# A fused attention and long-convolution kernel: a factored inverse transform, 1/sqrt in one pass, and output copies on ScalarE

## The chip, the cores and the metric

The kernel runs on one core of a Trainium2 chip. The metric is the device time of one execution in microseconds (us), as the median of several runs. The kernel before takes 247.82 us (3 runs, 247.66 to 248.04). All traces here have one core; the "granted clock" beside a run is the mean TensorE clock as a share of full speed, 0.989 for the profiled run of before. PE is the matmul engine, PEld its weight loads, DVE the vector engine, ACT the scalar engine, POOL is GpSimd. "L264" is line 264 of the kernel that is being profiled, so the same statement has slightly different line numbers in different kernels.

## The reference

```python
# q, k, v: (8 batches, 8 heads, 576, 64);   D = 64, S = 576, d_model = 512
kv  = einsum('bhsd,bhse->bhde', k, v)
out = einsum('bhsd,bhde->bhse', q, kv)
x   = out / sqrt(mean(out * out, -1) + 1e-6) * g_norm        # -> (8, 576, 512)
x1, x2, x3 = split(x @ w_proj, 3)                             # 512 x 1536
conv = irfft(rfft(x2) * rfft(filter_fft), n=576)              # along the sequence
y   = (x1 * conv * x3) @ w_out                                # 512 x 512
```

## The kernel before

The program loops over eight batches, and the work of batch b+1's attention (`att_o`, `att_r`, `att_x`, `fold`) is interleaved with batch b's transforms and projections. The forward and inverse transforms are matmuls against tables of cosines and sines; the radix-3 structure of 576 is used on the forward side (`fold`), not yet on the inverse. With cuts marked:

```python
def att_r(b, j):                     # 1/sqrt of the mean square, as exp(-0.5 * ln(.))
    r2 = ps_tile("ps_r2")
    ...                              # matmul: sums of squares into r2
    nc.scalar.activation(out=s['lr'][:, j % 2]..., in_=r2[...], func=AF.Ln, scale=1.0 / D, bias=bias_eps)
    if j % 2:
        nc.scalar.activation(out=s['rstd'][:, j - 1:j + 1], in_=s['lr'], func=AF.Exp, scale=-0.5)

def att_x(b, jp):                    # x = o * rstd, DVE, both inputs bf16 in SBUF
    nc.vector.tensor_mul(out=s['x'][:, r], in0=s['o'][:, r], in1=s['rstd'][:, r])
def fold(b, jp): ...                 # seven short DVE operations on x

def fft(b, g):
    ...                              # matmuls into a PSUM tile xp
    if g < 2:                        # tpw on DVE (PSUM input), the sum Y on POOL
        nc.vector.tensor_mul(out=t_[:n, 0], in0=xp[:n], in1=HH[:n, g, 1:3])
        nc.vector.tensor_mul(out=t_[:n, 1], in0=xp[:n], in1=HH[:n, g, 0:2])
        nc.gpsimd.tensor_add(out=Y[...], in0=t_[:n, :, 0], in1=t_[:n, :, 1])
        return
    nc.vector.tensor_mul(out=Y[:, 4:6], in0=xp[...], in1=HM)      # "the product Y"; frees xp

def inv(b, dcs):
    for h in (1, 0):
        for i, dc in enumerate(dcs):
            for g in range(3):       # three matmuls of 288 columns
                nc.tensor.matmul(p_[h][:, i], Y[...], IV[:n, 2 * g + h], start=(g == 0), stop=(g == 2))
    nc.scalar.copy(out=os_, in_=p_[1])
    nc.vector.tensor_add(out=u[:, :, 0:TH], in0=p_[0], in1=os_)
    nc.vector.tensor_sub(out=u[:, :, TH:S], in0=p_[0][:, :, ::-1], in1=os_[:, :, ::-1])
    nc.vector.tensor_mul(out=st[b]['yg'][:, d2], in0=u, in1=g13[:, d2])

def outp(b, c0, ev=None):            # output matmuls, then the copy from PSUM
    if c0 == 0 and not ev: nc.vector.tensor_copy(out=ot, in_=pp)
    else:                  nc.scalar.copy(out=ot[:, 0:n], in_=pp[:, 0:n])
```

In the traces here each engine takes its instructions one after another, in the order in which they were laid out. That order isn't the order of the Python text: a scheduler lays it out when the program is built, except where `keep_in_program_order` pins it. PSUM tiles come from a small shared pool, so a matmul into a new tile waits until an earlier tile has been read.

## Time and profile before

| what | before |
|---|---|
| time, median | 247.82 us |
| span of the profiled run | 246.6 us |
| busy share PE / DVE / ACT / POOL | 91 / 77 / 63 / 37 % |
| batch period, mean of five (starts of L264, 68.20 to 194.35) | 25.23 us (one short and one long: 25.34) |
| TensorE idle in a steady batch | 0.12 us |
| chain that ended last | PE 78 %, DVE 10 %, ACT 7 % |

The busy share of the whole span is an average over start, steady state and end. The period and the idle time within a batch say more: TensorE has nothing to spare, so what lengthens its in-order path lengthens the kernel. The period alternates between 24.8 and 25.9 us, because one output step is done for two batches at once. The lines themselves are in the prediction.

### The profile page before, as it was taken

Reading aid. Unit: us, or ns where it says so; the run is one execution under the profiler, and the core shown is the slowest. Engines: PE = TensorE matmul, PEld = TensorE weight load, DVE = VectorE, ACT = ScalarE, POOL = GpSimd, SP = SyncE. Lnnn points to the kernel's source line nnn. Section 1 sums busy time; section 2 is a strip of 40 time slices with the busy share of each in tenths; the row PEclk is TensorE's granted clock in tenths of the full one; section 3 lists DMA queues with packets and bytes.
Section 4 is the critical chain, followed back from the end, with each engine's and each line's share of the span. In section 5 each row is a group of like instructions: output and inputs, shape, how many; then the busy total and the mean of one; then the engine's idle time right before and its main releaser. Section 6 shows DMA issues by size and latency. Waiting matters only on the chain.

```text
span 246.6 us, 4887 instructions
## 1 busy us (share of the span) xinstructions
PE 225.6 (91%) x1964; PEld 133.9 (54%) x1964; DVE 190.7 (77%) x337; ACT 154.8 (63%) x231; POOL 90.8 (37%) x103
## 2 busy tenths in 40 slices
PE   4977896867999999999999999999999999999990
PEld 1433353434576657655766576557665766557520
DVE  6739866899698779876887888796779777958560
ACT  2856337981677767785679467946794679543430
POOL 7963992670193019400950086000700070007010
PEclk9999999997999999999999999999999999999998
DMA  6999999994099129914992389340033003400156
GB/s 68 166 196 238 211 194 196 192 180 50 4 142 211 43 64 135 211 49 112 104 185 85 88 98 177 100 129 3 4 85 85 3 0 88 128 0 3 39 151 193
DMA packets 45559, 27.17 MB, mean 110 GB/s; under 512 B 22274, under 2 KB 40706, under 8 KB 45538
## 3 DMA queue, kind: packets, MB, share of 16 engines
q0 software_dynamic: 40256, 17.70, 56.7%
q1 hardware_dynamic: 5122, 8.92, 13.2%
q8 instruction: 15, 0.25, 0.4%
q10 hardware_dynamic: 160, 0.26, 0.4%
q14 instruction: 6, 0.05, 0.1%
HBM read 33.69 MB, written 9.44 MB: 175 GB/s over the span
## 4 chain that ended last, share of the span: by engine, by line
PE 78%; DVE 10%; ACT 7%; issue 2%; ACTq 0%; DVEq 0%
PE ps_x L430 19%; PE ps_out L479 10%; PE ps_x L381 6%; PE ps_invo L454 5%; PE ps_inve L454 5%; PE ps_w L529 4%; PE ps_qT L247 3%; PE ps_o L264 3%; PE ps_x L387 3%; PE ps_x L372 3%; ACT sq L265 2%; PE ps_r L281 2%; PE ps_kv L223 2%; PE ps_x L375 2%; PE ps_X L407 2%
## 5 line engine op out<-in xcount | busy, mean ns | idle before, releaser
L430 PE MATMUL ps_x<-x,wp 128*128 128x288 bf16 x512 | 67.8, 286 | 0.2 <-ACT lr L282 0.2
L413 POOL TENSOR_TENSOR Y<-tpw 128x1024 bf16<-128x1024 f32 (+1 forms) x16 | 37.7, 2359 | 64.5 <-PE ps_r L281 39.7
L430 PEld LDWEIGHTS <-wp 128*128 128x128 bf16 x512 | 49.8, 98 | 14.0 <-issue 1.3
L265 ACT ACTIVATE sq<-ps_o 128x576 bf16<-128x576 f32 x32 | 20.6, 652 | 18.0 <-PE ps_o L264 18.0
L70 POOL DMA_DIRECT2D km<-in_k_dram x9 | 7.9, 873 | 63.2 <-PE ps_kv L223 63.2
L282 ACT ACTIVATE lr<-ps_r,bias_eps 128x576 f32<-128x576 f32 x32 | 23.4, 746 | 7.5 <-PE ps_r L281 7.4
L479 PE MATMUL ps_out<-wo,yg 128*128 128x512 bf16 x112 | 26.4, 379 | 0.7
L436 DVE TENSOR_TENSOR g<-ps_x,x 128x576 bf16<-128x576 f32 x32 | 24.1, 752 | 3.5 <-PE ps_x L430 2.3
L434 ACT CAST x<-ps_x 128x576 bf16<-128x576 f32 x32 | 20.6, 643 | 8.4 <-PE ps_x L430 8.4
L454 PEld LDWEIGHTS <-Y 128*128 128x128 bf16 (+1 forms) x192 | 19.0, 101 | 10.7 <-issue 3.1
L411 DVE TENSOR_TENSOR tpw<-ps_X,HH 128x1024 f32<-128x1024 f32 (+1 forms) x16 | 19.6, 1222 | 3.4 <-PE ps_X L409 2.5
L457 ACT COPY os<-ps_invo 128x576 f32<-128x576 f32 x14 | 9.0, 640 | 20.9 <-DVE u L460 16.3
L270 ACT ACTIVATE osb<-ps_o,g_col 128x576 bf16<-128x576 f32 x28 | 20.8, 741 | 0.0
L251 DVE COPY qT<-ps_qT 128x1152 bf16<-128x1152 bf16 x16 | 11.4, 752 | 11.1 <-PE ps_qT L247 11.1
L412 DVE TENSOR_TENSOR tpw<-ps_X,HH 128x1024 f32<-128x1024 f32 (+1 forms) x16 | 19.4, 1214 | 0.0
L285 ACT ACTIVATE rstd<-lr 128x1152 bf16<-128x1152 f32 x16 | 18.6, 1165 | 0.5
L479 PEld LDWEIGHTS <-yg 128*128 128x128 bf16 x112 | 10.9, 97 | 12.4 <-issue 1.9
L292 DVE TENSOR_TENSOR x<-osb,rstd 128x1152 bf16<-128x1152 bf16 x16 | 12.3, 766 | 6.9 <-ACT rstd L285 6.9
L381 PE MATMUL ps_x<-wp,ab 128*128 128x512 bf16 x64 | 15.5, 381 | 1.5 <-DVE ab L310 1.5
L454 PE MATMUL ps_invo<-IV,Y 128*128 128x288 bf16 (+1 forms) x84 | 13.7, 299 | 2.4 <-DVE g L436 1.6
L529 PE MATMUL ps_w<-kvblk,ind 128*128 128x512 bf16 x37 | 12.1, 469 | 3.8 <-DVE ind L103 3.4
L264 PE MATMUL ps_o<-qT,kvblk 128*128 128x288 bf16 x64 | 12.9, 288 | 2.8 <-DVE kvblk L232 1.7
(170 smaller groups left out, 395.4 us busy)
## 6 DMA issues: line engine op xcount, KB each, us to landing
out_dram<-ot SPq DMA_DIRECT2D x28, 256.0 KB, 3.3
qb<-in_q_dram POOLq DMA_DIRECT2D x16, 288.0 KB, 7.5
km<-in_k_dram POOLq DMA_DIRECT2D x7, 512.0 KB, 7.6
vm<-in_v_dram POOLq DMA_DIRECT2D x7, 512.0 KB, 9.7
wp<-in_moe_w_proj_dram POOLq DMA_DIRECT2D x3, 512.0 KB, 12.1
out_dram<-ot SPq DMA_DIRECT2D x10, 128.0 KB, 3.1
km<-in_k_dram POOLq DMA_DIRECT2D x2, 256.0 KB, 5.8
kt<-in_k_dram POOLq DMA_DIRECT2D x8, 64.0 KB, 6.7
```

The lines of the kernel that those rows point to most:

```text
L264: nc.tensor.matmul(op[:, h, 0:TH], kvblk[b % 2][:, j], s['qT'][:, 2 * (j % 2) + j // 2, h * TH:(h + 1) * TH], start=True, stop=True)
L265: nc.scalar.activation(out=s['sq'][:, j].rearrange("p (a b) -> p a b", a=2), in_=op[:, :, 0:TH], func=AF.Square)
L270: nc.scalar.activation(out=o_, in_=op[:, :, 0:TH], func=AF.Copy, scale=g_col)
L282: nc.scalar.activation(out=s['lr'][:, j % 2].rearrange("p (a b) -> p a b", a=2), in_=r2[:, :, 0:TH], func=AF.Ln, scale=1.0 / D, bias=bias_eps)
L381: nc.tensor.matmul(pp[:, h], ab[:, j, h * SB:h * SB + P], wp[:, j, DM:2 * DM], start=(j == 0), stop=(j == NDC - 1))
L413: nc.gpsimd.tensor_add(out=Y[:n, 2 * g:2 * g + 2], in0=t_[:n, :, 0], in1=t_[:n, :, 1])
L430: nc.tensor.matmul(pp[:, h, 0:TH], w_, x[:, j, h * TH:(h + 1) * TH], start=(j == 0), stop=(j == NDC - 1))
L434: nc.scalar.copy(out=x1, in_=pp[:, :, 0:TH])
L436: nc.vector.tensor_mul(out=st[b]['g13'][:, dc].rearrange("p (a b) -> p a b", a=2), in0=pp[:, :, 0:TH], in1=x1)
L454: nc.tensor.matmul(p_[h][:, i], Y[:n, 2 * g + h, dc * P:(dc + 1) * P], IV[:n, 2 * g + h], start=(g == 0), stop=(g == 2))
L479: nc.tensor.matmul(pp[:, cc], yg[:, dc, c * P:(c + 1) * P], wo[:, dc], start=(dc == 0), stop=(dc == NDC - 1))
L529: tc.keep_in_program_order(nc.tensor.matmul(pp[:, 0], ind, kvblk[1].rearrange("p a b -> p (a b)"), start=True, stop=True))
```

## The change

The intent: TensorE is the full engine, so give it less to do. The inverse of length 576 is factored: the matmuls now have 192 and 96 columns and give three parts of a third of the output each. DVE adds the short part (from the 96 columns, mirrored) to the two outer ones in one operation, and POOL makes the middle third, the short part less both outer ones, in two. The product that ends a batch's second half is moved behind the next batch's first projection (`fins[1]()`). To pay for the DVE work, an output copy goes to ScalarE, and to pay for that, 1/sqrt becomes one ScalarE pass.

```diff
-    preload_act_table_set("natural_log_exp_and_others")
+    preload_act_table_set("abs_reciprocal_sqrt_and_small")
@@ kv:  the second state eviction of the first batch moves to ScalarE
-            if b == 0:
+            if b == 0 and j0 == 0:
@@ att_r
-        activation(out=s['lr'][:, j % 2], in_=r2, func=AF.Ln, scale=1.0 / D, bias=bias_eps)
-        if j % 2:
-            activation(out=s['rstd'][:, j - 1:j + 1], in_=s['lr'], func=AF.Exp, scale=-0.5)
+        activation(out=s['rstd'][:, j], in_=r2, func=AF.Abs_reciprocal_sqrt, scale=1.0 / D, bias=bias_eps)
@@ inv
-                for g in range(3): matmul(p_[h][:, i], Y[...], IV[:n, 2 * g + h], ...)     # 288 columns
+                for g in (1, 2):   matmul(p_[h][:, i, 0:SB], Y[...], IV[:, 2 * g + h, 0:SB], ...)   # 192
+                matmul(p_[h][:, i, SB:TH], Y[:N1, h, cs], IV[:N1, h, 0:SB // 2], ...)               # 96
+        eng = eng or nc.gpsimd
+        eng.tensor_add(out=w3[:, :, 1], in0=u3[:, :, 0], in1=u3[:, :, 2])
+        eng.tensor_sub(out=w3[:, :, 1], in0=u3[:, :, 1], in1=w3[:, :, 1])
+        nc.vector.tensor_add(out=w3[:, :, 0:3:2], in0=u3[:, :, 0:3:2], in1=u3[:, :, 1:2].to_broadcast(...))
-        nc.vector.tensor_mul(out=st[b]['yg'][:, d2], in0=u, in1=g13[:, d2])
+        def fin(): nc.vector.tensor_mul(out=st[b]['yg'][:, d2], in0=w, in1=g13[:, d2])
+        return fin
@@ outp
-            if c0 == 0 and not ev: nc.vector.tensor_copy(out=ot, in_=pp)
-            else:                  nc.scalar.copy(out=ot[:, 0:n], in_=pp[:, 0:n])
+            nc.scalar.copy(out=ot[:, 0:n], in_=pp[:, 0:n])
@@ loop over batches
         proj2(b)
+        if b: fins[1]()
...
-        for dp in (0, 2): inv(b, (dp, dp + 1))
+        fins = [inv(b, (dp, dp + 1)) for dp in (0, 2)]
+        fins[0]()
```

Cut: a `warm(2)` left out at the start, and the last batch, which does all of this on DVE.

More of the change, by code (lines that the diff above doesn't have):

```diff
@@ L176 @@
         nc.scalar.activation(out=IV[:, 2 * c], in_=a_, func=AF.Sin, scale=cosb[:, 2 + h:3 + h], bias=cosb[:, h:h + 1])
-    tc.keep_in_program_order(nc.scalar.preload_act_table_set("natural_log_exp_and_others"))
+    tc.keep_in_program_order(nc.scalar.preload_act_table_set("abs_reciprocal_sqrt_and_small"))
     g_col = consts.tile([P, 1], FP32)
@@ L276, in att_r @@
             s['rstd'] = work.tile([P, NDC, S], BF16, name="rstd", tag="rstd")
-        if j % 2 == 0:
-            s['lr'] = work.tile([P, 2, S], FP32, name="lr", tag="lr")
         r2 = ps_tile("ps_r2")
@@ L281, in att_r @@
             nc.tensor.matmul(r2[:, h, 0:TH], ind, s['sq'][:, j, h * TH:(h + 1) * TH], start=True, stop=True)
-        nc.scalar.activation(out=s['lr'][:, j % 2].rearrange("p (a b) -> p a b", a=2), in_=r2[:, :, 0:TH], func=AF.Ln,
-                             scale=1.0 / D, bias=bias_eps)
-        if j % 2:
-            nc.scalar.activation(out=s['rstd'][:, j - 1:j + 1], in_=s['lr'], func=AF.Exp, scale=-0.5)
+        nc.scalar.activation(out=s['rstd'][:, j].rearrange("p (a b) -> p a b", a=2), in_=r2[:, :, 0:TH],
+                             func=AF.Abs_reciprocal_sqrt, scale=1.0 / D, bias=bias_eps)
     def att_x(b, jp):
@@ L436, in proj13, with inv @@
                 nc.vector.tensor_mul(out=st[b]['g13'][:, dc].rearrange("p (a b) -> p a b", a=2), in0=pp[:, :, 0:TH], in1=x1)
-    def inv(b, dcs):
+    def inv(b, dcs, eng=None):
         Y, g13 = st[b]['Y'], st[b]['g13']
@@ L451, in inv @@
             for i, dc in enumerate(dcs):
-                for g in range(3):
-                    n = N1 if g == 0 else P
-                    nc.tensor.matmul(p_[h][:, i], Y[:n, 2 * g + h, dc * P:(dc + 1) * P], IV[:n, 2 * g + h],
-                                     start=(g == 0), stop=(g == 2))
+                cs = slice(dc * P, (dc + 1) * P)
+                for g in (1, 2):
+                    nc.tensor.matmul(p_[h][:, i, 0:SB], Y[:, 2 * g + h, cs], IV[:, 2 * g + h, 0:SB],
+                                     start=(g == 1), stop=(g == 2))
+                nc.tensor.matmul(p_[h][:, i, SB:TH], Y[:N1, h, cs], IV[:N1, h, 0:SB // 2], start=True, stop=True)
         os_ = work.tile([P, 2, TH], FP32, name="os", tag="os")[:, 0:m]
@@ L460, in inv, with fin @@
         nc.vector.tensor_sub(out=u[:, :, TH:S], in0=p_[0][:, :, ::-1], in1=os_[:, :, ::-1])
+        eng = eng or nc.gpsimd
+        w = work.tile([P, 2, S], BF16, name="w", tag="w", bufs=2)[:, 0:m]
+        u3, w3 = (t.rearrange("p j (m r) -> p j m r", m=3) for t in (u, w))
+        eng.tensor_add(out=w3[:, :, 1], in0=u3[:, :, 0], in1=u3[:, :, 2])
+        eng.tensor_sub(out=w3[:, :, 1], in0=u3[:, :, 1], in1=w3[:, :, 1])
+        nc.vector.tensor_add(out=w3[:, :, 0:3:2], in0=u3[:, :, 0:3:2], in1=u3[:, :, 1:2].to_broadcast([P, m, 2, SB]))
         d2 = slice(dcs[0], dcs[0] + m)
-        nc.vector.tensor_mul(out=st[b]['yg'][:, d2], in0=u, in1=g13[:, d2])
+        def fin():
+            nc.vector.tensor_mul(out=st[b]['yg'][:, d2], in0=w, in1=g13[:, d2])
+        return fin
     yt = {}
@@ L469, in o_rows, with outp @@
         return bass.AP(tensor=out.tensor, offset=out.offset + (b * S + t0[0]) * DM, ap=[[3 * DM, 64]] + two + [[1, DM]])
-    def outp(b, c0, ev=None):
+    def outp(b, c0):
         if c0 < 4 or b % 2:
@@ L486, in outp @@
             n = 2 if c0 < 4 else 1
-            if c0 == 0 and not ev:
-                nc.vector.tensor_copy(out=ot, in_=pp)
-            else:
-                nc.scalar.copy(out=ot[:, 0:n], in_=pp[:, 0:n])
+            nc.scalar.copy(out=ot[:, 0:n], in_=pp[:, 0:n])
             for i in range(2):
@@ L516, in last @@
         for dc in range(NDC):
-            inv(b, (dc,))
+            inv(b, (dc,), nc.vector)()
             if dc < 2:
-                outp(b - 1, 2 * dc, nc.scalar.copy)
+                outp(b - 1, 2 * dc)
         act, dve = nc.scalar.copy, nc.vector.tensor_copy
@@ L536 @@
         kv(0, 2 * jj, 2 * jj + 2)
-        warm(2)
         att_o(0, 2 * jj)
@@ L549 @@
         proj2(b)
+        if b:
+            fins[1]()
         if b == 0:
@@ L602 @@
             del st[b - 1]
-        for dp in (0, 2):
-            inv(b, (dp, dp + 1))
+        fins = [inv(b, (dp, dp + 1)) for dp in (0, 2)]
+        fins[0]()
 _INS = ['q', 'k', 'v', 'g_norm', 'moe_w_proj', 'moe_filter_fft', 'moe_w_out']
```

## The prediction

> **What bounds the kernel now.** I read the page's busy shares first, then the busy time by stage, then the groups of instructions, then the order of time around the joint between two batches. On the page:
>
> ```profile
> span 246.6 us, 4887 instructions
> PE 225.6 (91%) x1964; PEld 133.9 (54%) x1964; DVE 190.7 (77%) x337; ACT 154.8 (63%) x231; POOL 90.8 (37%) x103
> ```
>
> TensorE leads, but a share over the span mixes start, steady state and end, so I cut the span at the starts of the inverse transform. Columns: window, length, then busy time (instructions) of PE, weight loads, DVE, ACT, POOL:
>
> ```profile
> 0.00:30.00 30.00, 22.66 (x176) 9.95 (x176) 21.42 (x68) 15.41 (x25) 21.86 (x46) 1.00 1.18 175
> 83.36:109.14 25.78, 25.66 (x240) 15.90 (x239) 21.75 (x36) 18.76 (x27) 9.32 (x8) 1.00 0.74 110
> 109.14:134.04 24.90, 24.77 (x233) 15.78 (x234) 19.87 (x34) 17.62 (x27) 9.32 (x8) 1.00 0.82 125
> ```
>
> In a steady batch TensorE idles 0.12 of 25 us: what shortens its work shortens the batch, and any new wait on its in-order path lengthens it. DVE, ACT and POOL have 4, 7 and 15 us to spare per batch. The groups of the instructions that change or show a price:
>
> ```profile
> L282 ACT ACTIVATE lr<-ps_r,bias_eps 128x576 f32<-128x576 f32 x32 | 23.4, 746 | 7.5 <-PE ps_r L281 7.4
> L265 ACT ACTIVATE sq<-ps_o 128x576 bf16<-128x576 f32 x32 | 20.6, 652 | 18.0 <-PE ps_o L264 18.0
> L285 ACT ACTIVATE rstd<-lr 128x1152 bf16<-128x1152 f32 x16 | 18.6, 1165 | 0.5
> L413 POOL TENSOR_TENSOR Y<-tpw 128x1024 bf16<-128x1024 f32 x8 | 18.9, 2362 | 62.3 <-PE ps_r L281 39.7 <-PE ps_X L404 19.1 <-DVE tpw L412 3.5
> L462 DVE TENSOR_TENSOR yg<-u,g 128x1152 bf16<-128x1152 bf16 x14 | 10.6, 758 | 0.5
> L488 DVE COPY ot<-ps_out 128x1024 f32<-128x1024 f32 x6 | 7.3, 1225 | 6.5 <-PE ps_out L479 6.5
> ```
>
> The chain that ended last gives TensorE's spacing: six inverse matmuls (288 columns) take 0.74 us, 0.1235 each; sixteen projection matmuls of 288 take 1.96; eight of 512 take 1.73, 0.216 each. That is about 2 ns plus 0.417 ns per column.
>
> Last, DVE against POOL in the first batch, in order of time (start, duration):
>
> ```profile
> 47.31 2.37 POOL L413 TENSOR_TENSOR Y<-tpw 128x1024 bf16<-128x1024 f32 x1 [2.24 <-DVE tpw L412]
> 49.32 0.98 DVE L292 TENSOR_TENSOR x<-osb,rstd 128x1152 bf16<-128x1152 bf16 x1
> 50.33 3.55 DVE L302 TENSOR_TENSOR d__687<-x 128x768 bf16<-128x768 bf16 x1
> 51.09 2.37 POOL L413 TENSOR_TENSOR Y<-tpw 97x1024 bf16<-97x1024 f32 x1
> ```
>
> The subtraction L302 takes 0.55 us everywhere else; here it takes 3.55 and ends 0.42 after POOL's add does. x takes 0.98 instead of 0.76 when it starts 0.36 before a POOL add ends. In the steady batches no DVE instruction with two SBUF inputs meets a POOL add: there the second add runs 98.82 to 101.17, DVE's next such instruction starts at 101.63, held off by the output copy L488 before it.
>
> **What the Trainium skill says.** *SBUF — State Buffer*, "Who interferes with whom": a DVE instruction with two SBUF inputs and a GpSimd instruction that reads SBUF exclude each other for the whole instruction; one with an input in PSUM is free. The two cases above agree (3.55 against 0.55), and products with a PSUM input run beside the same adds at their usual 1.21. *GPSIMD Engine Reference*, "Elementwise — side-by-side cycle accounting": about 2.6 cycles per element with two inputs; the trace has 2.36 us for 1024 elements, 2.3 ns each. *TensorE: Matmul & The Clock Gate*, "Back-to-back issue gap": columns / 2.4 GHz + 2.5 ns; agrees with the spacing above. The same section gives 81 ns for 128 columns with a weight load each; the table transposes (128x128 loads, 128 columns) take 0.36 us for six here, 60 ns, so the trace decides and loads stay hidden down to about there. *ScalarE: Activation LUTs*, "What ACT_TABLE_LOAD costs": every function has one price per element, and a pointer operand adds 93 ns; L282 against L265 (746, 652) agrees.
>
> **The change part by part.**
> Inverse: per batch 24 matmuls of 288 columns (24 x 0.1235 = 2.96 us) become 16 of 192 (0.0825) and 8 of 96 (0.042): 1.66 us. A load limit of 60 ns on the 96-column ones would add 0.15. Saving 1.3 us per batch, all on TensorE: 9.1 us for the seven batches outside the last.
> Middle third: for each of two pairs per batch, POOL does two operations on 384 elements, DVE one on 768. An estimate from the 2.36 us add and the skill's per-element rate: 0.9 to 1.0 us per POOL operation, 4 us per batch. DVE's is priced by L302: 0.55, 1.1 per batch, against the 1.22 output copy that leaves it.
> 1/sqrt: four passes with a bias pointer, about 0.74 each, replace 4 x 0.746 + 2 x 1.165: ACT falls by 2.3 us per batch and takes a 1.01 us output copy. ACT is not the bound; but in the start it is on the path. There the second x begins at 23.66, after lr (20.63 to 22.00) and rstd (22.04 to 23.20), and the second state eviction waits on DVE until 18.32. Without the two Exp passes and with that eviction on ACT at about 17.2, x begins near 21.2. Start: -2.4 us. The later start-up chain (filter products on ACT and DVE) is unchanged and should pass this on.
> End: four single inverses with everything on DVE. Per column block DVE takes 0.46 + 0.45 + 0.25 + 0.25 + 0.46 plus some of a 0.35, about 2.1 us against 1.36 between the last two products before. It eats the 1.3 us that TensorE saves there: +0.4.
> Gross: 247.8 - 9.1 - 2.4 + 0.4 = 236.7, if nothing new waits.
>
> **What waits anew: the joint.** The static order of the changed kernel has, on DVE: both u of pair 1, w, both u of pair 2, product 1, w, product 2, and only then the two qT copies of the next batch. In the trace of before TensorE meets that copy here:
>
> ```profile
> 91.75 1.42 DVE L251 COPY qT<-ps_qT 128x1152 bf16<-128x1152 bf16 x2 [1.30 <-PE ps_qT L247]
> 93.00 0.42 PE L264 MATMUL ps_o<-qT,kvblk 128*128 128x288 bf16 x2
> ```
>
> Count from the start of the inverse (83.36). Before, the copy starts at 8.4 and L264 at 9.64. After, TensorE is there at 8.34. rstd comes 1.2 us earlier, so the folds end at 1.5 and the first u pair at 3.1; pair 2 (single os buffer, 0.64 us of ACT between) ends at 5.2. Free of the lock, POOL ends its second pair at 5.2 + 0.16 + 2 x 1.0 + 0.1 = 7.5, product 2 ends at 8.3, the copy at 9.0: TensorE stands 0.7 us (0.4 after even batches, whose inverse starts later). With the lock, w, two POOL operations and the product of each pair are serial: 2 x (0.5 + 2.0 + 0.7) = 6.4 us from 3.1 plus gaps of 0.4, then the copy 0.7: 10.6, a stall of 2.2, more than the 1.3 saved.
>
> **What waits anew: the third block.** The output copy that held x off is gone from DVE. x is ready 2 us earlier, at 99.5 in the old clock, and meets the POOL add until 101.17. The static order now also puts the seven folds (1.9 us) in front of the Y product that frees the PSUM tile which L430 takes at 103.76. 101.2 + 0.65 + 1.9 + 1.15 = 104.9: a stall of 1.2 to 1.5 in each of six batches. Without the lock it ends at 103.2, no stall.
>
> **Rivals.**
> (a) All hidden: 236.7. For it: TensorE was the only full engine and the deferred product shows that the joint was thought of. Against: the copy behind product 2.
> (b) POOL in series but hardly blocked: five joints x 0.5, the first joint (its product 1 stands before pair 2) +1, the last +0.3: 240.5. For it: the two lock cases are from one batch, and POOL on bf16 is not in this trace; at 0.6 us per operation the joint almost closes.
> (c) Lock at the joint: 236.7 + 5 x 2.1 + 3 + 1 = 251.
> (d) Lock there and in the third block: + 6 x 1.4 = 259.6. For it: the arithmetic above. Against: DVE might come first at some meetings, and each figure rests on overlaps of some tenths.
>
> **Range and chances.** By the trace alone I would lean to (c) or (d). But they need several meetings to fall badly, and POOL's duration is an estimate on which a third of the stall hangs. I weigh (a) 0.12, (b) 0.28, (c) 0.33, (d) 0.27, with spread around each. The middle is 248.5; eight in ten lie between 238.5 and 260. Faster by over 2% (under 242.9): 0.28; within 2%: 0.36; slower (over 252.8): 0.36.
>
> **What would show it.** The inverse groups at 0.083 and 0.042 spacing, 1.66 us per batch (right up to 1.8). The new ACT group near 740 ns. POOL operations on 384 elements at 0.9 to 1.0 when unblocked, longer in some instances. L264 after the joint waiting 0.4 to 2.2 us on the qT copy. x of the third block stretched to over 2 us and a projection matmul waiting on the Y product. The prediction is wrong if these waits are absent (then 237), if the mean POOL operation is under 0.6, or if the start gains nothing because a load lands late.

## The result, and the profile after

The changed kernel is correct and takes 255.17 us (4 runs, 254.42 to 256.17) against 247.79 us for before (4 runs). The ratio is 1.0299, with a 95 % interval of 1.0255 to 1.0343: slower. All ratios in this text are the mean time of one kernel's fast runs over that of the other's in the same rounds, so they are not quite the ratios of the medians quoted. The profiled spans are 254.2 and 246.6 us.

The head of the profile page, and the chain that ended last, by engine:

```profile
span 254.2 us, 4875 instructions
PE 214.6 (84%) x1932; PEld 130.0 (51%) x1960; DVE 208.6 (82%) x355; ACT 143.5 (56%) x223; POOL 119.2 (47%) x131
...
DVE 45%; PE 25%; POOL 12%; ACT 5%; DMA 5%; issue 5%; DVEq 0%; POOLq 0%
```

TensorE has about 11 us less to do, as intended (28 matmul records are missing from this trace, 1932 against 1960 weight loads, so the true figure is somewhat smaller), and the span is 7.6 us longer. The chain has left TensorE: it was 78 % of it before, it is 25 % now, and DVE and POOL carry 57 %. Busy time by stage, cut again at the starts of the inverse (the columns are those of the same view in the prediction):

```profile
86.53:113.75 27.22, 24.59 (x238) 15.45 (x239) 24.59 (x40) 17.56 (x26) 13.67 (x12) 1.00 0.71 104
113.75:139.25 25.50, 23.30 (x230) 15.14 (x233) 22.57 (x33) 16.40 (x26) 13.66 (x12) 1.00 0.80 122
```

TensorE now idles 2.2 to 2.6 us a batch (missing records count as idle; the two waits named below make 1.8 to 2.3 of it) where it idled 0.12, and DVE is busy 22.6 to 24.6 us where it was busy 19.9 to 21.8. The groups that changed or showed a price:

```profile
L280 ACT ACTIVATE rstd<-ps_r,bias_eps 128x576 bf16<-128x576 f32 x32 | 23.3, 742 | 11.8 <-PE ps_r L279 11.8
L288 DVE TENSOR_TENSOR x<-osb,rstd 128x1152 bf16<-128x1152 bf16 x16 | 21.1, 1317 | 2.7 <-ACT rstd L280 2.6
...
L469 DVE TENSOR_TENSOR yg<-w,g 128x1152 bf16<-128x1152 bf16 x14 | 14.8, 1056 | 5.3 <-POOL w L464 4.7
```

A mean hides what goes on here. yg, with the same shape as before (758 ns), has a mean of 1056: its median is still 758, its longest instance takes 1455. x has a mean of 1317 for the same operation that took 766 before: its median is 760, its longest 2293. Something stretches some instances. What TensorE waited for, from the view of waits (total, times, longest):

```profile
PE ps_o L264 <- DVE qT L251: 7.2, 6, 2.2
PE ps_x L426 <- DVE Y L415: 6.1, 6, 1.1
...
PE ps_x L426 <- DVE FX L210: 2.4, 1, 2.4
```

None of the three is in that view of before. They are the three places of the whole story: the joint between two batches (L264 on the copy qT), the third block of a batch (L426 on the product Y), and the start (L426 on the table copy FX).

**The joint.** The timeline of the changed kernel from the inverse of one batch (starts at 113.75) to the first attention product of the next; start, duration, engine, and in brackets the idle time before it. Only rows of DVE and POOL are shown, and the one of TensorE at the end:

```profile
116.51 0.56 DVE L465 TENSOR_TENSOR w<-u 128x768 bf16<-128x768 bf16 x1
116.55 1.28 POOL L463 TENSOR_TENSOR w<-u 128x384 bf16<-128x384 bf16 x1 [11.63 <-DVE u L459]
...
117.93 0.75 DVE L459 TENSOR_TENSOR u<-ps_inve,os 128x576 bf16<-128x576 f32 x1
118.79 0.91 POOL L463 TENSOR_TENSOR w<-u 128x384 bf16<-128x384 bf16 x1
...
118.86 1.45 DVE L469 TENSOR_TENSOR yg<-w,g 128x1152 bf16<-128x1152 bf16 x1 [0.18 <-POOL w L464]
119.78 1.31 POOL L464 TENSOR_TENSOR w<-u,w 128x384 bf16<-128x384 bf16 x1
120.24 1.26 DVE L465 TENSOR_TENSOR w<-u 128x768 bf16<-128x768 bf16 x1
121.60 0.76 DVE L469 TENSOR_TENSOR yg<-w,g 128x1152 bf16<-128x1152 bf16 x1
122.28 1.42 DVE L251 COPY qT<-ps_qT 128x1152 bf16<-128x1152 bf16 x2
123.08 0.40 PE L264 MATMUL ps_o<-qT,kvblk 128*128 128x288 bf16 x2 [0.74 <-DVE qT L251]
```

Read it as a relay. w and POOL's first addition start together at 116.5, and POOL takes 1.28 instead of 0.91. The u at 117.93, which reads PSUM, runs beside POOL at its usual 0.75. Then yg and POOL's addition start within 0.07 us: yg takes 1.45. POOL's next one takes 1.31 beside it, then w takes 1.26. The second yg (0.76) still stands in the queue, and only then is DVE free for the copy that TensorE is waiting for. From 116.51 to 122.28 DVE's operations on SBUF alone and POOL's have taken turns.

**The third block.** DVE's order before the change (the folds follow from 129.31):

```profile
126.37 1.22 DVE L488 COPY ot<-ps_out 128x1024 f32<-128x1024 f32 x1 [1.09 <-PE ps_out L479]
127.51 0.75 DVE L292 TENSOR_TENSOR x<-osb,rstd 128x1152 bf16<-128x1152 bf16 x1
128.18 1.22 DVE L419 TENSOR_TENSOR Y<-ps_X,HM 128x1024 bf16<-128x1024 f32 x1
```

And in the changed kernel, some 6 us after the joint above:

```profile
129.14 2.36 POOL L409 TENSOR_TENSOR Y<-tpw 97x1024 bf16<-97x1024 f32 x1
129.85 2.27 DVE L288 TENSOR_TENSOR x<-osb,rstd 128x1152 bf16<-128x1152 bf16 x1 [0.19 <-ACT rstd L280]
...
134.05 1.22 DVE L415 TENSOR_TENSOR Y<-ps_X,HM 128x1024 bf16<-128x1024 f32 x1
...
135.32 2.12 PE L426 MATMUL ps_x<-x,wp 128*128 128x288 bf16 x16 [1.08 <-DVE Y L415]
```

x ends at 132.12, 0.62 after POOL's addition does at 131.50; its work takes 0.76 where nothing meets it, so most of the 2.27 us was standing. The cut lines between x and Y are the seven folds, 1.9 us in all. Y is what frees the PSUM tile that the projection matmul needs.

**The start.** DVE and TensorE near the first projections:

```profile
27.56 1.15 PE L426 MATMUL ps_x<-x,wp 128*128 128x288 bf16 x8
...
29.09 1.23 DVE L318 TENSOR_TENSOR ff<-fa,fc 128x1024 bf16<-128x1024 f32 x1 [3.74 <-DMA fc<-in_moe_filter_fft_dram,fidx]
...
30.80 0.29 DVE L210 COPY FX<-ps_ft 64x256 bf16<-64x256 bf16 x1
...
31.14 4.57 PE L426 MATMUL ps_x<-x,wp 128*128 128x288 bf16 x24 [2.43 <-DVE FX L210]
```

TensorE is at the projections at 27.56 instead of 30.03, so the gain of the shorter 1/sqrt arrives there. But DVE's next instruction, ff, waits for a gathered load until 29.09, and behind it stand two table copies whose data has long been ready and which free a PSUM tile. TensorE has run into a queue that it used to arrive at just late enough not to notice.

The queue takes back the 2.47 us, and a second loss comes on top. The 24 projection matmuls behind the wait take 4.57 us. In e12, an experiment below with the same start, they take 3.10 after nearly the same wait:

```profile
30.59 3.10 PE L426 MATMUL ps_x<-x,wp 128*128 128x288 bf16 x24 [2.08 <-DVE FX L210]
```

The granted clock differs: from 31 to 36 us it is 0.68 in the changed kernel and 1.00 in e12 and in before. Among the seven kernels with this start, the three with 4.5 to 4.8 us (changed, e7, e11) have 0.68 to 0.72 there, after waits of 2.0 to 3.7 us; the four with 3.10 have 1.00, after 1.3 to 2.1 us. Whether the wait brings the lower clock on isn't shown: e12 waited 2.08 us and kept the clock, e11 waited 2.03 and did not. The wait and the clock together make the filter's transform start 1.6 us later than before (35.55 for 33.96).

The 7.6 us of span add up from the starts of L264: up to the first joint 2.2 us are lost (70.36 against 68.20), in the five periods after it 5.2 us (26.27 against 25.23 each), and 0.3 in the rest. In a period the inverse saves 1.2 us (2.98 to 1.70 and 1.81 by turns), the joint costs 0.99 (7.2 less the first 2.25, over five) and the third block 1.05; 0.2 us remain for smaller waits.

### The profile page after: what moved, and what is told of

It reads as the page before. It is cut to its first block, busy times and chain, and to the rows that moved or that the text cites. A ratio compares the mean times of both kernels' runs of the same rounds, so it can differ in the third digit from the quotient of the medians.

```text
span 254.2 us, 4875 instructions
## 1 busy us (share of the span) xinstructions
PE 214.6 (84%) x1932; PEld 130.0 (51%) x1960; DVE 208.6 (82%) x355; ACT 143.5 (56%) x223; POOL 119.2 (47%) x131
## 4 chain that ended last, share of the span: by engine, by line
DVE 45%; PE 25%; POOL 12%; ACT 5%; DMA 5%; issue 5%; DVEq 0%; POOLq 0%
PE ps_x L426 14%; DVE x L288 6%; DVE yg L469 6%; DMA fc<-in_moe_filter_fft_dram,fidx 5%; POOL w L463 4%; DVE tpw L408 4%; DVE tpw L407 4%; PE ps_out L487 3%; DVE Y L415 3%; DVE w L465 3%; POOL w L464 3%; ACT rstd L280 3%; DVE u L458 3%; DVE u L459 2%; DVE g L432 2%
## 5 line engine op out<-in xcount | busy, mean ns | idle before, releaser
L426 PE MATMUL ps_x<-x,wp 128*128 128x288 bf16 x512 | 69.7, 290 | 9.2 <-DVE Y L415 6.1
L426 PEld LDWEIGHTS <-wp 128*128 128x128 bf16 x512 | 50.3, 99 | 26.2 <-issue 12.5
L463 POOL TENSOR_TENSOR w<-u 128x384 bf16<-128x384 bf16 x14 | 15.7, 1124 | 76.1 <-DVE u L459 76.1
L280 ACT ACTIVATE rstd<-ps_r,bias_eps 128x576 bf16<-128x576 f32 x32 | 23.3, 742 | 11.8 <-PE ps_r L279 11.8
L487 PE MATMUL ps_out<-wo,yg 128*128 128x512 bf16 x99 | 25.8, 379 | 0.7
L495 ACT COPY ot<-ps_out 128x1024 f32<-128x1024 f32 (+1 forms) x17 | 15.9, 937 | 14.0 <-PE ps_out L487 14.0
L288 DVE TENSOR_TENSOR x<-osb,rstd 128x1152 bf16<-128x1152 bf16 x16 | 21.1, 1317 | 2.7 <-ACT rstd L280 2.6
L469 DVE TENSOR_TENSOR yg<-w,g 128x1152 bf16<-128x1152 bf16 (+1 forms) x18 | 16.6, 922 | 5.4 <-POOL w L464 4.7
L264 PE MATMUL ps_o<-qT,kvblk 128*128 128x288 bf16 x64 | 12.8, 287 | 9.6 <-DVE qT L251 7.2
L79 POOL DMA_DIRECT2D qb<-in_q_dram x16 | 12.6, 786 | 7.3 <-DMA wp<-in_moe_w_proj_dram 4.1
L464 POOL TENSOR_TENSOR w<-u,w 128x384 bf16<-128x384 bf16 x14 | 15.1, 1080 | 1.1
L279 PE MATMUL ps_r<-sq,ind 128*128 128x288 bf16 x64 | 13.1, 286 | 1.4 <-ACT osb L270 0.8
```

The lines of the kernel that those rows point to most:

```text
L280: nc.scalar.activation(out=s['rstd'][:, j].rearrange("p (a b) -> p a b", a=2), in_=r2[:, :, 0:TH], func=AF.Abs_reciprocal_sqrt, scale=1.0 ...
L426: nc.tensor.matmul(pp[:, h, 0:TH], w_, x[:, j, h * TH:(h + 1) * TH], start=(j == 0), stop=(j == NDC - 1))
L463: eng.tensor_add(out=w3[:, :, 1], in0=u3[:, :, 0], in1=u3[:, :, 2])
L464: eng.tensor_sub(out=w3[:, :, 1], in0=u3[:, :, 1], in1=w3[:, :, 1])
L469: nc.vector.tensor_mul(out=st[b]['yg'][:, d2], in0=w, in1=g13[:, d2])
L487: nc.tensor.matmul(pp[:, cc], yg[:, dc, c * P:(c + 1) * P], wo[:, dc], start=(dc == 0), stop=(dc == NDC - 1))
```

## The experiments

Twelve kernels ran, on two chips, each beside runs of the kernel before. "Period" is the mean of the five steps from the third batch's first L264 to the last batch's. The granted clock over a whole run scatters (0.978 to 0.985 in the four runs of the changed kernel), and some of the scatter of the times goes with it: in e11 the run at 0.995 took 246.16 us and the one at 0.977 took 249.58.

| run | what it is | median us (before, same rounds) | ratio, 95 % interval |
|---|---|---|---|
| e1 | whole change but the inverse | 251.47 (248.11) | 1.0152, 1.0104 to 1.0200 |
| e2 | changed, tables first at the start | 253.27 (248.11) | 1.0216, 1.0148 to 1.0284 |
| e3 | changed, products behind qT | 250.76 (248.11) | 1.0146, 1.0073 to 1.0220 |
| e4 | changed, four folds behind Y | 253.39 (248.11) | 1.0223, 1.0130 to 1.0316 |
| e5 | before, output copies alone | 245.60 (247.93) | 0.9906, 0.9834 to 0.9978 |
| e6 | before, 1/sqrt alone | 259.48 (247.93) | 1.0490, 1.0409 to 1.0571 |
| e7 | changed, Y right behind x | 248.86 (247.93) | 1.0019, 0.9942 to 1.0096 |
| e8 | changed, all three orders | 240.55 (247.93) | 0.9692, 0.9624 to 0.9760 |
| e9 | e1 with the two orders that apply | 241.62 (247.66) | 0.9761, 0.9730 to 0.9793 |
| e10 | e8 with the middle third on DVE | 240.65 (247.66) | 0.9716, 0.9689 to 0.9743 |
| e11 | changed, middle third on DVE | 247.80 (247.66) | 0.9996, 0.9940 to 1.0053 |
| e12 | changed, POOL only writes (wrong result) | 246.62, one run (247.66) | none |

All but e12 gave the right result. One run each of e1 and e4 is left out of the ratios.

### e1: the change without its inverse

```diff
-    (new inv, fins)
+    (inv of the kernel before, product straight from u)
```

> The changed kernel with the old inverse put back (no middle third, no GpSimd work, product straight from u); everything else of the change stays. Theory (the loss is the inverse's DVE/GpSimd side): batches go back to about 25.3 us between the first attention products of neighbouring batches (26.4 after, 25.3 before), the waits on qT and on Y vanish (under 0.2 us a batch), and the time is 247 to 249 us: the before-time, less about 1.3 us gained by ScalarE in the first batch, plus the 1.6 us that the start got longer. Rival (the output copies or the 1/sqrt on ScalarE hold something up): 252 us or more, with a period over 26 us.

The theory fell here. I had put the loss on the inverse. The time lies between the theory's 247 to 249 and the rival's 252, but the period is the rival's. Without it the wait on qT is gone, but the third block still waits 6.3 us on Y, six times 1.05, and the kernel is 1.5 % slower than before with a period of 26.14 us. So of the 3 % about half has nothing to do with the inverse, its matmuls or its GpSimd work.

### e5 and e6: the two ScalarE parts, each alone on the kernel before

```diff
 e5:
-            if c0 == 0 and not ev: nc.vector.tensor_copy(out=ot, in_=pp)
-            else:                  nc.scalar.copy(out=ot[:, 0:n], in_=pp[:, 0:n])
+            nc.scalar.copy(out=ot[:, 0:n], in_=pp[:, 0:n])
 e6:
-        Ln pass, and an Exp pass for every second one
+        activation(out=s['rstd'][:, j], in_=r2, func=AF.Abs_reciprocal_sqrt, ...)
```

> The kernel before with one part of the change alone: its output copies on ScalarE. In its order DVE has x, then the product Y, then the seven folds, as before, only without the copy. Theory (after the first four runs: what costs 1.05 us in each of six batches is the order x, folds, Y, which the shorter 1/sqrt brings about, and not the place of the copy): no wait on Y in the third block, period 25.3 us, time within 1 % of before, 246 to 249 us. Rival (the copy on ScalarE, or DVE without the copy, makes x meet GpSimd's addition and that alone costs the microsecond): a wait of 0.5 to 1.1 us on Y in six batches, 250 to 254 us.

> The kernel before with one other part alone: 1/sqrt in one ScalarE pass. DVE's order becomes x, seven folds, the output copy, and Y last. Theory (the faster 1/sqrt makes x come first, and the work that the scheduler then puts ahead of Y holds the PSUM tile): Y comes about 1.1 us later still than in the run without the new inverse, so the wait on Y is 2.0 to 2.5 us in six batches and the time 257 to 262 us, though the change takes work from ScalarE and adds none anywhere. Rival (ScalarE's shorter chain is free time, and the third block is only held by x's meeting with GpSimd): 246 to 249 us, or at most the 1.05 us a batch of the run without the inverse, 252 to 254 us.

Both came out as the theory had it. The copies alone are 0.9 % faster. The shorter 1/sqrt alone, which takes 2.3 us a batch from ScalarE and adds nothing anywhere, makes the kernel 4.9 % slower, more than the whole change does. The timeline of e6 in the third block shows why:

```profile
126.95 2.34 POOL L409 TENSOR_TENSOR Y<-tpw 97x1024 bf16<-97x1024 f32 x1
127.66 2.25 DVE L288 TENSOR_TENSOR x<-osb,rstd 128x1152 bf16<-128x1152 bf16 x1
...
131.83 1.22 DVE L484 COPY ot<-ps_out 128x1024 f32<-128x1024 f32 x1
132.96 1.22 DVE L415 TENSOR_TENSOR Y<-ps_X,HM 128x1024 bf16<-128x1024 f32 x1
133.10 0.41 PE L264 MATMUL ps_o<-qT,kvblk 128*128 128x288 bf16 x2 [0.75 <-DVE ot L484]
...
134.23 1.02 PE L426 MATMUL ps_x<-x,wp 128*128 128x288 bf16 x7 [0.73 <-DVE Y L415]
```

Before, DVE's order was copy, x, Y, folds. With 1/sqrt earlier the program is laid out as x, folds, copy, Y. The work that nobody waits for yet (folds) stands in front of the two instructions that free PSUM tiles (copy, Y), and x, now early, stands beside POOL's addition and takes 2.25 us. TensorE waits 0.39 + 0.75 + 0.73 us in each of six batches, 11.2 of the 11.5 us, and the period is 27.3 us. (The 0.39 us is a wait for a tile that ScalarE's osb frees. That tiles are short there because the copy stands late is argued, not tested; nor was e6 itself run in another order. e7 below tests the order in the changed kernel.) In e5 the order is x, Y, folds, and x comes when POOL's addition is nearly over (1.05 us); nothing waits.

### e4 and e7: the order in the third block

```diff
 e4: fold(b + 1, 0) called after fft(b, 2) in the program
 e7: the same, and x, Y and the first two folds pinned in that order
+            if nxt and dc == 2: fold(b + 1, 0)
+        tc.keep_in_program_order(...)     # on x, on the product Y, on the first two folds
```

> Only the order in the third block: four of the seven fold operations of DVE come after the product Y instead of before it. Theory (six batches lose 1.1 us each because Y, which frees the PSUM tile of a projection, stands behind x and seven folds): the wait on Y falls under 0.3 us while x stays near 2.3 us, and the time falls by 5 to 6.5 us to 249 to 250 us. Rival (the folds are then late for the next projection, or the joint's wait grows by what the third block gives back, because DVE has no slack): a new wait on rr, ab or qT of 0.5 to 1 us in each batch, time 253 us or more.

> The changed kernel with DVE's order in the third block fixed as x, Y, then all seven folds. Theory: x keeps its 2.2 to 2.3 us (it still meets GpSimd's addition), but the waits on Y (6 x 1.1 us) and the one that took their place when only four folds were moved (6 x 0.7 us) are both under 0.2 us; 249 to 250.5 us. Rival (the lock's stretch of x is itself the loss): the wait on Y or at the r2 tile stays above 0.5 us a batch, 252 us or more.

In e4 four of the seven folds went behind Y, and Y came some 1 us earlier after x, but the wait did not vanish: it moved to another tile of the pool. The view of waits names it (the waits on qT, 7.2 us, are as in the changed kernel):

```profile
PE ps_r L279 <- DVE Y L415: 3.8, 6, 0.7
```

6.1 us of waits became 3.8, and the time of 253.39 us, with wide scatter, is the rival's rather than the theory's 249 to 250. With Y pinned right behind x (e7) both waits are gone, x still takes up to 2.29 us, and the time is 248.86 us. So in e7 the stretch of x brings no wait by itself. It costs through what stands behind it.

### e3: the order at the joint

```diff
-        if b: fins[1]()
...
-        fins[0]()
+        elif nxt: kv(b + 1); qtr(b + 1); fins[0](); fins[1]()
+        # the qT copies and the two products pinned in this order
```

> Both products yg of a batch are put behind the two qT copies in DVE's order; the same work, the same GpSimd operations. Theory (the joint is held by DVE's order: qT waits behind a product that waits for GpSimd): the waits of the attention product on qT (2.2, 1.2, 0.7, 1.2 us ...) fall under 0.3 us, third-block waits stay near 1.1 us, time 247 to 250 us. Rival 1 (DVE's serial work is simply too long, the wait moves on to the next thing behind the products, tpw and Y): the wait on Y grows from 1.1 to about 2 us, and the time stays within 1.5 us of 255.2. Rival 2 (the joint is set by the lock itself, u and w are stretched): the qT wait only halves, 252 us.

The waits on qT vanish entirely (7.2 us to none; L264 waits 0.2 us on rstd instead). The third block's waits grow from 6.1 to 10.1 us, which is rival 1's move: what the joint holds back no longer, DVE still has to do before Y. The time, 250.76 us, lies just past the theory's range, and by the ratios (1.0146 against 1.0299) about 3.8 us are gained, between the two. But little of that is in the steady batches: the period is 26.10 us for 26.27, so there the wait mostly moved, as rival 1 has it. The gain in the profile lies before the third L264 (64.82 for 70.36), in the first joint and in a start whose filter load landed earlier and whose clock stayed at 1.00, which the edit does not touch.

### e11 and e12: is it the order alone, or the meetings of DVE and GpSimd?

```diff
 e11:
-        eng = eng or nc.gpsimd
+        eng = eng or nc.vector
 e12 (wrong result on purpose):
-            eng.tensor_add(...); eng.tensor_sub(...)
+            eng.tensor_copy(out=junk[:, 0:1], in_=u[:, 0, 0:1]);  eng.memset(junk, 0.0)        # 128 x 1024 fp32
+            eng.tensor_copy(out=w3[:, 0, 1, 0:1], in_=junk[:, 0:1]);  eng.memset(w3[:, :, 1], 0.0)
```

> The changed kernel with its orders as they are, the middle third on DVE. Theory (what the joint waits for is DVE's serial work up to qT, lengthened by stretched w and yg from 6.3 to about 7.2 us): the waits on qT fall from 7.2 us in all to 1 to 4 us, the third block's stay at 1.1 us each since GpSimd's addition for Y still meets x, and the time is 250 to 253 us. Rival (the lock is not it, DVE's order alone is): the waits on qT stay at 7 us or grow, as DVE has four more operations in front of qT, 255 us or more.

> Wrong result on purpose: GpSimd's two operations of the inverse are replaced by memsets (with a one-column copy ahead that waits for u, so that they run at the same place), so GpSimd writes and hardly reads beside DVE's w and yg. Theory (w, yg and x are stretched because GpSimd's two-input operation holds something that DVE's two-input operations on bf16 in SBUF need too): w takes 0.56 us and yg 0.76 us in every place in the seven joints, though GpSimd is busy beside them, while x in the third block, beside the untouched addition, still takes 2.2 to 2.3 us. Rival (any GpSimd activity in SBUF stretches them, or the profile counts a wait for GpSimd's result as DVE's time): w or yg of 1.2 us or more in several batches.

e11 gives DVE four more operations a batch, all in front of the qT copy, and the kernel gets 3 % faster than the changed one: 247.80 us, better than the 250 to 253 expected. The waits on qT fall from 7.2 to 1.0 us, those on Y stay (6.5 us). Every w and yg takes its 0.55 and 0.75 us. In this order the help of GpSimd cost more than doing the work on DVE.

e12 keeps GpSimd busy in the same place and takes all its reads away but those of one column. In the timeline, POOL and DVE side by side:

```profile
113.27 0.95 POOL L465 MEMSET junk<- 128x1024 f32 x1
114.29 0.52 POOL L466 CAST w<-junk 128x1 bf16<-128x1 f32 x1
```

```profile
113.54 0.75 DVE L475 TENSOR_TENSOR yg<-w,g 128x1152 bf16<-128x1152 bf16 x1
114.20 0.55 DVE L471 TENSOR_TENSOR w<-u 128x768 bf16<-128x768 bf16 x1
```

yg takes 0.75 us although a memset of 0.95 us runs beside it; the longest yg of the whole run is 0.759 and the longest w 0.559, while x in the third block still takes up to 2.29 beside the untouched addition. The one GpSimd instruction that reads, a copy of one column, shows the other side: it takes 0.19 us elsewhere, and 0.52 here, ending at 114.81 just after w does at 114.75. The Trainium skill's page *SBUF — State Buffer*, "Who interferes with whom", says that a DVE instruction with two SBUF inputs contends with a GpSimd instruction that reads SBUF, and not with one that only writes it. This run agrees in both halves.

### e2: the order at the start

```diff
-            nc.vector.tensor_copy(out=FW[:n, a], in_=d[:, 0:6])
+            tc.keep_in_program_order(nc.vector.tensor_copy(out=FW[:n, a], in_=d[:, 0:6]))
             # and the same for the three FX copies: all of them ahead of ff
```

> Only the order of DVE at the start: all copies of the transform tables FW and FX before the filter's ff additions. Theory (the in-order queue of DVE hides the start's gain): the 2.4 us wait of PE in the first gating projections vanishes, the filter's transform starts near 33.0 instead of 35.4 us, and the whole kernel gets 2.0 to 2.5 us faster, 252.7 to 253.2 us. Rival (a load, or ff being later, holds the start anyway): the filter's transform starts at 35 us or later and the time stays within 0.5 us of 255.2.

The wait is gone. The filter's transform starts at 30.95 us, earlier than the 33.0 expected, and the time of 253.27 us is within a tenth of the range. The gain in the whole is uncertain on its own scale (intervals of 0.7 %), but the trace isn't: in the six other runs with the changed kernel's start (e1, e3, e4, e7, e11, e12) that point lies at 32.5 to 35.7 us, depending on when the gathered filter load lets ff start (27.5 to 29.3 us) and on whether the clock falls there; in the four with the tables first it lies between 30.9 and 31.2 whatever the load does (27.4 to 28.5). Of the 4.6 us that e2 gains in the start, 1.3 are lost again one batch later: the granted clock from 65 to 70 us is 0.66 (1.00 in the changed kernel), just after the joint's wait of 2.25 us, and that batch takes 27.45 us instead of 26.13.

### e8, e9 and e10: everything in order

e8 is the changed kernel with the edits of e2, e3 and e7 together. e9 is e1 with the edits of e2 and e7. e10 is e8 with the edit of e11.

> The three order fixes together on the changed kernel: tables before ff at the start, both products behind the qT copies, Y right behind x. Same work as the changed kernel, the same GpSimd operations. Theory (only order loses the gain, DVE has slack enough): PE's waits in the middle batches fall under 0.3 us a batch, the period is 24.0 to 24.3 us (25.34 of before less 1.27), time 238 to 242 us, 2 to 4 % faster than before. Rival (DVE with the lock's stretches has no slack left, and the wait moves to tpw, g13 or u): period above 25 us, 245 us or more.

> The old inverse with everything else of the change and with the two order fixes that still apply (tables first at the start, Y right behind x). Against the run with the three orders it has the new inverse alone taken out. Theory (with the order mended, the inverse pays what TensorE saves, less what small waits remain): period 25.0 to 25.1 us as in the run with the copies alone, time 243 to 245 us, so that the inverse is worth 3 to 4 us (its 1.27 us a batch less 0.6 of small waits, times seven, less what the first and last batch lose). Rival (the inverse's DVE and GpSimd work eats its gain even in the right order): 240 to 242 us, no more than 1 us from the run with the three orders.

> The three orders, and the middle third worked out by DVE in place of GpSimd: GpSimd has nothing of the inverse. Theory (GpSimd's help at the joint is worth about nothing, since w and yg wait for it or are stretched beside it): yg takes 0.75 us and w 0.55 us everywhere, DVE gets four more operations of 0.35 us each a batch, and the time is that of the three orders within 1 us, 239.5 to 241.5 us. Rival 1 (the lock's stretch is the dearer): 239 us or less. Rival 2 (DVE has no slack, every operation more is on the path): 243 us or more.

e8 does the same work as the changed kernel and takes 240.55 us, 3.1 % less than before: it beats both kernels. The span of its profiled run is 239.1 us, and its chain is:

```profile
PE 52%; DVE 32%; issue 4%; ACT 4%; POOL 3%; DMA 2%; POOLq 0%; DVEq 0%; ACTq 0%
```

The chain is on TensorE again, though not by 78 %. The period is 24.7 us, not the 24.0 to 24.3 that I expected. e9 shows how little the inverse itself is worth even then: without it, and in order, the kernel takes 241.62 us, so the inverse brings about 1 us (e10 against e9, same chip and rounds: 240.65 against 241.62; e8 against e9, by their ratios, 1.7 us, with intervals that overlap). My theory for e9, 3 to 4 us, fell; the rival had it. Where the rest goes can be read by setting one batch of e8 against the same batch of e9. From its first L264 to the next e9 takes 25.58 us and e8 25.28 (87.78 to 113.06). The inverse is 1.28 us shorter (1.71 for 2.99). The second L264 comes 3.45 us after the first instead of 3.12 (it waits for rstd), the projection behind it 0.14 later, and the r2 matmul behind the third projection 0.40 later (it waits for Y):

```profile
91.23 0.41 PE L264 MATMUL ps_o<-qT,kvblk 128*128 128x288 bf16 x2 [0.18 <-ACT rstd L280]
...
98.92 0.42 PE L279 MATMUL ps_r<-sq,ind 128*128 128x288 bf16 x2 [0.24 <-DVE Y L421]
```

That is 0.87 of the 0.98 us. x takes 2.68 us in that batch, so Y is late even right behind it. e10, with no GpSimd in the inverse at all, comes to the same time as e8, as expected (ratios 0.9716 and 0.9692, intervals overlap): once the order leaves room, the meetings at the joint cost nothing that these runs resolve, and GpSimd's help gains nothing either.

## Why the prediction was right or wrong

The measured 255.17 us lies in the range, and "slower" was one of the two outcomes given 0.36; the predicted 248.5 is 6.7 us low. It was a weighted middle of four rivals, of which (d), both locks, 259.6, is what happened; the mechanisms of (d) were right and three terms of its sum were mis-sized: the joint, the third block and the start. They erred in both directions, so that (d) comes within 4.4 us of the measured time is in part luck.

- **Inverse on TensorE: right.** 1.66 us a batch predicted, 1.70 to 1.81 measured. The 96-column matmuls did not hit the 60 ns load limit that was feared: in e8 one with its own weights starts at 104.71 and the next matmul at 104.75.
- **Prices of the operations: right.** rstd 742 ns (about 740 predicted), POOL's additions 0.91 us when nothing blocks them (0.9 to 1.0 predicted), 1.28 to 1.31 when something does.
- **The joint: the mechanism right, the size off.** "a stall of 2.2" was meant for the ordinary joint, which shows 0.7 and 1.2 by turns, mean 0.99; the first joint, for which the sum has 3, shows 2.25. The relay was counted as 2 x (0.5 + 2.0 + 0.7) plus 0.4, 6.8 us; it took 5.8 (116.51 to 122.28), as two POOL operations take 1.82 unblocked rather than 2.0 and the pairs overlap. Over six joints that is 7.2 us instead of 2.1 x 5 + 3 = 13.5, and the 1 us for the last pair does not show: TensorE has no wait over 0.15 us from 213.74 to 243.73. e11 and e12 show the lock, e3 shows the order.
- **The third block: right, with one cause missed.** 1.2 to 1.5 us predicted in each of six batches, 1.02 measured (0.88 to 1.10). The prediction's own sum gives less than it says: 104.9 less 103.76 is 1.1. But the stall was put down to "the output copy that held x off is gone", and the order with the folds ahead of Y was taken as given. e5 and e6 show that the copy's move does no harm (0.9906) and that the earlier 1/sqrt is what reorders the folds (1.049).
- **The start: wrong.** "Start: -2.4 us" failed in its last clause, "is unchanged and should pass this on". The 2.4 us arrive at the first projections (27.56 for 30.03) and are lost on DVE's queue, where ff waits for a load with table copies behind it. In the profiled run the filter's transform starts 1.6 us later than before instead of 2.4 earlier, as the clock then takes another 1.5 us (4.57 for 3.10), which no part of the prediction has. The prediction named this way of failing, a load that lands late, but the load is only part of it; e2 shows that the order behind it is another.
- **The end: right in size.** +0.4 predicted; from the last batch's first inverse matmul to the end of the span it is 18.56 us before and 18.68 after, +0.1.
- **A reading of the lock that stays half open.** Of the 3.55 us of L302, the first 0.76 lie before POOL's addition starts (50.33 against 51.09), longer than its work of 0.55. The addition cannot have held it in that time; what did, isn't shown.

Put into (d)'s sum: 236.7, plus 4.0 for the start (from -2.4 to +1.6 in the profiled run), plus 7.2 and 6.1 for the two stalls, is 254.0, against 256.17 for the profiled run, whose waits these are (the median is 255.17). That start scatters by 3 us between profiles.

What stays open: what brings the lower clock on in the start, why before itself has a period 0.2 us longer than e5, with no wait in its view that would say so, and whether the 0.87 us a batch that e8 loses to rstd and Y can be had as well.

## What to carry to other kernels

When an engine's work is made shorter, ask which in-order queues its results pass next, and read the new static order: here a faster 1/sqrt, alone, cost 4.9 %, as the scheduler then put seven unhurried instructions in front of two that free PSUM tiles. Put what frees a buffer or feeds the full engine first in its queue, pin that order, and only then judge the change: the same work took 255.2 us in one order and 240.6 in another. Before giving a neighbour engine part of a chain, check that its reads don't exclude the very instructions that it is meant to relieve; here it cost 3 % in one order, and was worth nothing in the other.

## What the Trainium skill lacked or had wrong

- *SBUF — State Buffer*, "Who interferes with whom" has the rule right but doesn't say how it looks in a profile: the blocked instruction is shown as running, with the wait inside its duration and no releaser (x at 2.27 us for 0.76 us of work, ending 0.62 us after POOL's addition).
- *GPSIMD Engine Reference*, "Elementwise — side-by-side cycle accounting" gives a rate per element and names a dispatch cost for GpSimd without a figure. At 2.6 cycles and 1.2 GHz, 384 elements are 0.83 us and 1024 are 2.22; the runs show 0.907 to 0.914 unblocked (bf16) and 2.36 (fp32), 6 to 10 % more, which is not a fixed part alone.
- *TensorE: Matmul & The Clock Gate*, "Back-to-back issue gap" gives some 81 ns for a matmul of 128 columns and 131 ns for one of 512 in a stream where each has its own weights. Here the table transposes of 128 columns (before, 26.97 to 27.25) start 55 ns apart and the output matmuls of 512 columns 216 ns, each with its own weights. The 24 matmuls of the new inverse take 1.70 us, 71 ns on average at 192 and 96 columns, and in e8 the one after a matmul of 96 columns (104.71) started 0.04 us after it.
- No page says that a program's static order on an engine can change when an operation elsewhere gets shorter; in e6 that was the whole effect, 11.5 us.
